# Eight columns' 47 rows end to end in three tiles of 128, a start without Nyquist DMAs, no clamp in the weights' conversion, and a new order of the steps

## The chip, the cores and the metric

One core of a Trainium2 chip. The time is the device time of one execution in microseconds (us). Matmuls run on TensorE (PE in the profile; PEld is its loading of weights), elementwise work on VectorE (DVE), ScalarE (ACT) and GpSimd (POOL), and most DMAs are issued by SyncE (SP). "fp32r" is the reduced form of float32 in which the large matmuls run.

## The reference

```python
# x: (8, 3008, 256) float32
X = np.fft.fft(x, axis=1)
X = np.fft.fft(X, axis=2)
h = X.real.astype(np.float32).reshape(8 * 3008, 256) @ w_in      # 256 -> 2048
g = np.where(h >= 1, h, np.where(h <= -1, 0.0, (h + 1) ** 2 / 4))
out = g @ w_out                                                  # 2048 -> 256
```

So: the real part of a two-dimensional Fourier transform of each batch, then a feed-forward layer with a piecewise activation. `w_in` and `w_out` arrive as float64, whose bits the kernel itself turns into float32.

## The kernel before

The transform over 3008 = 64 x 47 rows is done in two stages of matmuls. The host only rearranges x: row numbers become pairs (a of 64, b of 47), and each of eight tiles per batch holds 16 columns' values and their mirrored ones (the two halves of the tile's middle axis), which are added before stage 1 since only the real part of the result is wanted.

**Stage 1** (`stage1(b, q)`, L258, one call for each of 8 tiles q of batch b): `fold_x` adds the two halves on GpSimd (L129); for batch 0's first tile TensorE accumulates both halves instead. A tile has 96 partitions: two groups of 47 rows, each padded to 48. Four fp32 matmuls (L270) contract them with a block matrix `bm` of two cosine and sine blocks, 96 columns each, into one PSUM bank. Tile 0 has one more small matmul (L275) for the Nyquist column. Four copies of 64x192 carry the bank into `z` (L281 on VectorE for odd q of batch 0, L283 on ScalarE otherwise). **Stage 2** (`stage2(b, h)`, L308, six calls) contracts over the 64 and splits the result into high and low fp32r halves `pqh` (ScalarE, L165) and `pql` (VectorE, L166). `nyquist(b)` (L288) makes 24 rows of 64 for the Nyquist column; they go to DRAM, and `nyquist_rows` (L300) loads each of three chunks back, spread over 128 partitions. Batch 0 uses ScalarE's DMA queue for the first of these, the other batches SyncE's.

The rest of the transform over 256 is folded into the weights: `fold_w_in(f4, m)` (L233) multiplies the converted `w_in` by cosine or sine matrices (fp32 matmuls of 512 columns, L237) and splits the result into `wh` and `wl`; the sine half's first row becomes `delta`, which goes through DRAM to lie across partitions (`fold_delta`, L254; group 0 on ScalarE's queue).

**Conversion of weights.** There are 16 jobs of 128x512 float64 values: jobs 0, 1, 4, 5, 8, 9, 12, 13 of `w_in`, the others of `w_out`. `magnitude(n)` (L188) scales the high word on ScalarE (L199, by 2^112) and the low word (L201, or VectorE at L210 for jobs 0 and 1). `assemble(n)` (L204) clamps the scaled word from below (L211), shifts and merges the low word (L212), and puts the sign in (L214). Jobs from 6 on keep the scaled word in the PSUM bank that the transform also uses. `split_w_out(n)` (L220) makes high and low halves of `w_out`, the low one on GpSimd for jobs 2 and 3 and on VectorE for the others.

**Units.** Batch b, chunk k of 3 (482 or 512 columns) and feature tile f of 16 make one unit: `gemm1` (six fp32r matmuls, L368), then `us` and two `h` on VectorE (L371 to L374), relu and square on ScalarE (L381, L382), the larger of two on VectorE (L383), the high half `gh` on ScalarE (L384), the low half `gl` on GpSimd (L387), and four units later (`LAG`) `gemm2` (twelve matmuls, L411, into four accumulator banks). There are 48 units to a batch, 384 in all. Batch 0 goes over its chunks twice, for the first and then the last eight feature tiles.

**Order.** `LOADS` is the order of SyncE's first loads (the first two raws on ScalarE's queue), `START` the order on the four compute engines before unit 0, and `STEPS` what is added before a unit of batch 0. Letters: c converts (e and v: its two functions by themselves), p a piece of the transform of batch 0 (0 to 7 stage 1, 8 the Nyquist rows, 9 to 14 stage 2), a and b the two halves of a fold, o a split of `w_out`, l a load of a raw, k the clearing of a row, w filling matmuls, r `fold_delta` and the Nyquist rows. For the first four units TensorE keeps program order; elsewhere a scheduler places instructions by priority and its own model. Each later batch's transform of 15 pieces is spread over the units of the batch before it; in batch 0 it begins at unit `FIRST_DFT`, and its loads at `FIRST_LOAD`.

## Time and profile before

| | us |
|---|---|
| median of three runs | 1760.84 (1759.97 to 1761.49) |
| the profiled execution | 1763.07 |
| its span, first to last instruction | 1761.3 |

In the profile a row of the timeline has its start, its duration, engine, line and operation, the tile written and the tiles read, a count, and in brackets how long its engine was idle before it and what ended that. A row of a group has the count, the busy time and the mean duration in ns, then the idle time before it and its releasers. A row of the stages has the stretch, its length, each engine's busy time with the number of its instructions in brackets, the granted clock of TensorE, and the DMAs. Matmuls are pipelined: durations overlap, and the distance of two starts is what one of them costs.

### The profile page before, as it was taken

Reading aid. Unit: us, or ns where it says so; the run is one execution under the profiler, and the core shown is the slowest. Engines: PE = TensorE matmul, PEld = TensorE weight load, DVE = VectorE, ACT = ScalarE, POOL = GpSimd, SP = SyncE. Lnnn points to the kernel's source line nnn. Section 1 sums busy time; section 2 is a strip of 40 time slices with the busy share of each in tenths; the row PEclk is TensorE's granted clock in tenths of the full one; section 3 lists DMA queues with packets and bytes.
Section 4 is the critical chain, followed back from the end, with each engine's and each line's share of the span. In section 5 each row is a group of like instructions: output and inputs, shape, how many; then the busy total and the mean of one; then the engine's idle time right before and its main releaser. Section 6 shows DMA issues by size and latency. Waiting matters only on the chain.

```text
span 1761.3 us, 21722 instructions
## 1 busy us (share of the span) xinstructions
PE 1731.3 (98%) x7894; PEld 1413.0 (80%) x7894; DVE 1415.2 (80%) x1706; ACT 1351.2 (77%) x1587; POOL 1209.8 (69%) x853
## 2 busy tenths in 40 slices
PE   8999999999999999999999999999999999999999
PEld 4766788888888888888888888888888888888877
DVE  5888788788887887878877788777888778888887
ACT  5777877787777877787777877778778787777776
POOL 3556867876668766677666876677666766667775
PEclk9999999999999999999999999999999999999999
DMA  7023321110010100110001100011000001000000
GB/s 230 22 73 103 104 99 43 37 53 31 1 52 27 53 31 1 60 41 31 31 9 52 50 28 25 33 37 49 20 25 34 1 23 35 8 25 6 18 25 25
DMA packets 32084, 72.54 MB, mean 41 GB/s; under 512 B 5092, under 2 KB 10340, under 8 KB 31976
## 3 DMA queue, kind: packets, MB, share of 16 engines
...
q14 instruction: 46, 0.38, 0.1%
...
## 4 chain that ended last, share of the span: by engine, by line
PE 78%; ACT 4%; POOL 4%; DVE 3%; issue 2%; ACTq 0%; POOLq 0%
PE acc L411 49%; PE uv L368 24%; POOL gl L387 3%; DVE h L383 3%; PE s L270 2%; PE s L318 2%; ACT gh L384 2%; ACT a L382 2%; ACT a L381 1%; ACT z L283 0%; POOL y L129 0%; DVE h L373 0%; DVE h L374 0%; PE ny L290 0%; PE s L275 0%
## 5 line engine op out<-in xcount | busy, mean ns | idle before, releaser
L387 POOL TENSOR_TENSOR gl<-h,gh 128x512 fp32r<-128x512 f32 (+1 forms) x765 | 1089.1, 1447 | 491.7 <-ACT gh L384 435.0
L383 DVE SCALAR_TENSOR_TENSOR h<-a,h 128x1024 f32<-128x1024 f32 (+1 forms) x385 | 586.0, 1522 | 224.8 <-ACT a L382 223.1
L384 ACT ACTIVATE gh<-h 128x1024 fp32r<-128x1024 f32 (+1 forms) x385 | 400.7, 1041 | 349.3 <-DVE h L383 337.3
L411 PE MATMUL acc<-gh,woh 128*128 128x512 f32 (+1 forms) x1536 | 610.7, 398 | 7.2 <-ACT gh L384 4.6
L411 PE MATMUL acc<-gl,woh 128*128 128x512 f32 (+1 forms) x1536 | 605.0, 394 | 6.9 <-POOL gl L387 6.7
L411 PE MATMUL acc<-gh,wol 128*128 128x512 f32 (+1 forms) x1536 | 600.5, 391 | 0.0
L381 ACT ACTIVATE a<-h,half 128x1024 f32<-128x1024 f32 (+1 forms) x385 | 431.5, 1121 | 20.4 <-DVE h L374 18.4
L382 ACT ACTIVATE a<-a 128x1024 f32<-128x1024 f32 (+1 forms) x385 | 398.9, 1036 | 7.3
L411 PEld LDWEIGHTS acc<-gl,woh 128*128 128x128 f32 x1536 | 289.8, 189 | 75.0 <-POOL gl L387 14.4
L411 PEld LDWEIGHTS acc<-gh,woh 128*128 128x128 f32 x1536 | 290.2, 189 | 69.8 <-ACT gh L384 6.7
L411 PEld LDWEIGHTS acc<-gh,wol 128*128 128x128 f32 x1536 | 290.3, 189 | 59.6 <-issue 1.2
L373 DVE TENSOR_TENSOR h<-us,uv 128x512 f32<-128x512 f32 (+1 forms) x384 | 259.5, 676 | 67.2 <-POOL gl L387 26.6
L368 PE MATMUL uv<-pqh,wh 128*128 128x512 f32 (+1 forms) x768 | 302.8, 394 | 2.1 <-DVE h L374 1.4
L368 PE MATMUL uv<-pql,wh 128*128 128x512 f32 (+1 forms) x768 | 301.3, 392 | 0.0
L368 PE MATMUL uv<-pqh,wl 128*128 128x512 f32 (+1 forms) x768 | 300.4, 391 | 0.0
L371 DVE SCALAR_TENSOR_TENSOR us<-nyb,delta,uv 128x512 f32<-128x512 f32 (+1 forms) x384 | 278.8, 726 | 23.3 <-PE uv L368 18.3
L374 DVE TENSOR_TENSOR h<-us,uv 128x512 f32<-128x512 f32 (+1 forms) x384 | 256.2, 667 | 0.0
L368 PEld LDWEIGHTS uv<-pqh,wh 128*128 128x128 f32 x768 | 145.1, 189 | 40.9 <-DVE h L374 5.7
L368 PEld LDWEIGHTS uv<-pql,wh 128*128 128x128 f32 x768 | 144.9, 189 | 30.9 <-DVE pql L166 0.4
L368 PEld LDWEIGHTS uv<-pqh,wl 128*128 128x128 f32 x768 | 145.1, 189 | 29.7
L129 POOL TENSOR_TENSOR y<-x 96x512 f32<-96x512 f32 x56 | 100.2, 1789 | 11.1 <-PE s L270 7.5
L283 ACT ACTIVATE z<-s 64x192 f32<-64x192 f32 x240 | 81.3, 339 | 8.6 <-PE s L275 3.5
...
## 6 DMA issues: line engine op xcount, KB each, us to landing
x<-in_x_dram SPq DMA_DIRECT2D x64, 384.0 KB, 3.4
...
```

The costliest lines, as they stand in the source:

```text
L129: nc.gpsimd.tensor_tensor(y, t[:, 0], t[:, 1], op=ALU.add)
L283: nc.scalar.activation(dst, src, AF.Copy)
L368: nc.tensor.matmul(t[:, :n], w[m][:, cols], r[:, m, :n], start=(j == 0), stop=(j == 2))
L371: nc.vector.scalar_tensor_tensor(us, nyb[b, k][:, :n], delta[:, f : f + 1], uv[0], op0=ALU.mult, op1=ALU.add)
L373: nc.vector.tensor_tensor(h[:, 0], us, uv[1], op=ALU.subtract)
L374: nc.vector.tensor_tensor(h[:, 1], us, uv[1], op=ALU.add)
L381: nc.scalar.activation(a[:, sl], h[:, sl], AF.Relu, bias=half, scale=0.5)
L382: nc.scalar.activation(a[:, sl], a[:, sl], AF.Square)
L383: nc.vector.scalar_tensor_tensor(h[:, sl], a[:, sl], 1.0, h[:, sl], op0=ALU.min, op1=ALU.max)
L384: nc.scalar.activation(gh[:, sl], h[:, sl], AF.Copy)
L387: eng.tensor_tensor(gl[:, sg], h[:, sg], gh[:, sg].bitcast(F32), op=ALU.subtract)
L411: nc.tensor.matmul(acc[:, :n], w[:, f, wc], g[:, sg], start=(first and j == 0), stop=(last and j == 2))
```

## The change

1. **Stage 1.** Eight columns' 47 rows lie end to end, 376 rows in three tiles of 128 partitions. Each of three matmuls covers the columns that have rows in its tile: 3, 4 and 3 of them, 144, 192 and 144 outputs that overlap in the bank and accumulate there. A tile of x is 128 x 2 x 384 instead of 96 x 2 x 512.
2. **Batch 0's first Nyquist rows.** `nyquist_spread` makes chunk 0's rows on 128 partitions by eight matmuls whose stationary operand is one column of `z` repeated; `first_delta` turns group 0's row by four matmuls of one partition. The DMAs for these go, and so does ScalarE's queue: all loads are SyncE's.
3. **Conversion.** ScalarE scales by 2^-112, the clamp goes, and the sign is put in by another pair of bit operations. `w_out` results of jobs from 6 on are written into the raw tile, and all splits of `w_out` take GpSimd.
4. **Order.** New `LOADS`, `START` and `STEPS`; steps come after a unit's first half instead of before it; TensorE no longer keeps program order in the first units; batch 1's loads and transform begin at units 24 and 28 instead of 21 and 25.

```diff
+KT = 3
+XW = KT * P
+SPANS = [(k * P // NBB * 2 * NC, (min((k + 1) * P, 8 * NBB) - 1) // NBB * 2 * NC + 2 * NC) for k in range(KT)]
+BM = np.cumsum([0] + [hi - lo for lo, hi in SPANS])
...
-LOADS = "x0 l0 x1 l1 m0 x2 x3 x4 x5 x6 x7 l4 l5 l2 l3 l6 l7"
-START = "c0 c1 p0 w2 p1 p8 b0 p2 p3 p4 p5 p6 r0 e4 p7 k0 a0 p9 p10 e5 v4 e2 v5 v2 e3 v3"
-NEXT = ""
-MANUAL_UNITS = 4
+LOADS = "l0 x0 l1 m0 x1 x2 x3 x4 x5 x6 x7 l4 l5 l2 l3 l6 l7"
+START = "e0 v0 e1 v1 p0 b0 a0 p1 p8 p2 d0 p3 p4 p5 p6 e4 v4 p7 s0 p9 p10 e5 v5 k0 b1 e2 v2 e3 v3"
 STEPS = {
-    0: "o2",
-    1: "b1 a1 o3 p11",
-    2: "p12",
-    3: "p13 p14 l8 l9",
-    4: "c6 o6",
-    5: "c7 o7",
-    6: "l10",
-    9: "c8",
-    11: "c9 l11",
-    13: "b2 a2 c10 o10 l12",
-    15: "c11 o11 l13",
-    17: "c12 l14",
-    19: "c13 l15",
-    20: "c14 o14",
-    21: "b3 a3",
-    22: "c15 o15",
+    0: "a1 o2",
+    3: "o3",
+    4: "p11 e6 v6 l8 l9",
+    5: "p12",
+    6: "o6 e7 l12",
+    7: "v7 p13",
+    8: "o7",
+    9: "p14 e8",
+    10: "v8 l13",
+    11: "c9",
+    13: "b2",
+    14: "a2",
+    15: "c12 l10",
+    16: "l11",
+    17: "c13",
+    18: "l14",
+    19: "b3",
+    20: "a3",
+    21: "c10 l15",
+    22: "o10",
+    23: "c11",
+    24: "o11",
+    25: "c14",
+    26: "o14",
+    29: "c15",
+    30: "o15",
 }
-FIRST_LOAD, FIRST_DFT = 21, 25
+FIRST_LOAD, FIRST_DFT = 24, 28
...
-POOL_JOBS = (2, 3)
-LEAST = float(2.0**97)
+POOL_JOBS = (2, 3, 6, 7, 10, 11, 14, 15)
-SCALAR_LOADS = 2
+VECTOR_COPIES = (2, 4, 6)
...
-        pin(nc.scalar.activation(t, high.bitcast(F32), AF.Abs, scale=2.0**112))
+        pin(nc.scalar.activation(t, high.bitcast(F32), AF.Abs, scale=2.0**-112))
...
-        eng.tensor_scalar(t, t, LEAST, None, op0=ALU.max)
         nc.vector.scalar_tensor_tensor(bits, bits, 3, low, op0=ALU.logical_shift_left, op1=ALU.bitwise_or)
-        w = f32s.setdefault(n, t).bitcast(U32)
-        nc.vector.scalar_tensor_tensor(w, high, 0x7FFFFFFF, bits, op0=ALU.bitwise_or, op1=ALU.bitwise_and)
+        if n not in f32s:
+            f32s[n] = low.bitcast(F32)
+        w = f32s[n].bitcast(U32)
+        nc.vector.scalar_tensor_tensor(w, high, 0x80000000, bits, op0=ALU.bitwise_and, op1=ALU.bitwise_or)
...
+    def first_delta():
+        t = drows[0]
+        pt = fft_bank(0, "dps")[:, : 4 * NA].rearrange("p (i n) -> p i n", i=4)
+        for i in range(4):
+            nc.tensor.matmul(pt[:, i], t[:, i * P : (i + 1) * P], half[:1].to_broadcast([1, NA]), start=True, stop=True)
+        nc.scalar.activation(delta[:, :4], pt[:, :, 0], AF.Copy, scale=2.0)
...
-        for i in range(GPC):
+        for k, (lo, hi) in enumerate(SPANS):
             for j, part in enumerate(y):
-                lhs = part[:, i * P : (i + 1) * P]
-                mm = nc.tensor.matmul(pt[:, i], lhs, bm[:96, :], start=(j == 0), stop=(j == len(y) - 1))
+                at = k, j
+                mm = nc.tensor.matmul(
+                    pt[:, lo:hi],
+                    part[:, k * P : (k + 1) * P],
+                    bm[:, BM[k] : BM[k + 1]],
+                    start=at == (0, 0),
+                    stop=at == (KT - 1, len(y) - 1),
+                    skip_group_check=True,
+                )
...
-                if b == 0 and q % 2:
+                if b == 0 and q in VECTOR_COPIES:
                     nc.vector.tensor_copy(dst, src)
...
+    def nyquist_spread():
+        pt = fft_bank(0, "nys").rearrange("p (c d) -> p c d", d=NA)
+        for c in range(8):
+            lhs = zt[0][:, c, P : P + 1].to_broadcast([P, P])
+            nc.tensor.matmul(pt[:, c], lhs, rm[:, :NA], start=True, stop=True)
+        nyb[0, 0] = sb.tile([P, CH], F32, tag="nyb", name="nyb_0_0", bufs=4)
+        nc.scalar.activation(nyb[0, 0].rearrange("p (c d) -> p c d", d=NA), pt, AF.Copy)
...
             gemm1(i)
+            activate(i)
+            run_steps(STEPS.get(i, ""))
```

More of the change, by code (lines that the diff above doesn't have):

```diff
@@ L140, in fft_ffn_kernel @@
     bm, rm = (cs[:, _OFF[i] : _OFF[i + 1]] for i in range(2))
-    cm = sb.tile([P, _OFF[6] - _OFF[2]], F32, tag="y", name="cm", bufs=3)
+    cm = sb.tile([P, _OFF[6] - _OFF[2]], F32, tag="nyb", name="cm", bufs=4)
     mats = [[cm[:, (2 * m + h) * P : (2 * m + h + 1) * P] for h in range(2)] for m in range(2)]
@@ L183, in load_w @@
             src = w_out[at[0] * m : (at[0] + 1) * m, :].bitcast(U32).rearrange("(f p) x -> p f x", p=P)
-        queue = nc.scalar if n < SCALAR_LOADS else nc.sync
-        queue.dma_start(raw.rearrange("p e two -> p (e two)").rearrange("p (f x) -> p f x", f=src.shape[1]), src)
+        nc.sync.dma_start(raw.rearrange("p e two -> p (e two)").rearrange("p (f x) -> p f x", f=src.shape[1]), src)
         raws[n] = raw
@@ L242, in fold_w_in @@
         nc.scalar.activation(t, pt[:1, :], AF.Copy)
-        drows[f4] = dr.tile([1, CH], F32, tag="drow", name=f"drow_{f4}", bufs=2)
-        (nc.sync if f4 else nc.scalar).dma_start(drows[f4], t)
+        drows[f4] = t
+        if f4:
+            row = dr.tile([1, CH], F32, tag="drow", name=f"drow_{f4}", bufs=2)
+            nc.sync.dma_start(row, t)
+            nc.sync.dma_start(delta[:, f4 * 4 : f4 * 4 + 4], row.rearrange("o (i p) -> p (o i)", p=P))
         split(wh[m][:, cols], wl[m][:, cols], pt)
@@ L252, in clear_row @@
             nc.gpsimd.memset(w[1][:1, f4 * CH : (f4 + 1) * CH].bitcast(F32), 0.0)
-    def fold_delta(f4):
-        row = drows.pop(f4).rearrange("o (i p) -> p (o i)", p=P)
-        (nc.sync if f4 else nc.scalar).dma_start(delta[:, f4 * 4 : f4 * 4 + 4], row)
+    def first_delta():
[4 more added lines that the diff above has]
+        nc.scalar.activation(delta[:, :4], pt[:, :, 0], AF.Copy, scale=2.0)
     def stage1(b, q):
@@ L294, in nyquist @@
         row = dr.tile([NC, NA], F32, tag="row", name=f"nyr_{b}", bufs=2)
-        (nc.sync if b else nc.scalar).dma_start(row, t)
+        nc.sync.dma_start(row, t)
         rows[b] = row
-        if b:
-            nyquist_rows(b, range(NCHUNK))
+        nyquist_rows(b, range(0 if b else 1, NCHUNK))
+    def nyquist_spread():
[5 more added lines that the diff above has]
+        nc.scalar.activation(nyb[0, 0].rearrange("p (c d) -> p c d", d=NA), pt, AF.Copy)
     def nyquist_rows(b, ks):
@@ L369, in gemm1, with hidden @@
             uv.append(t[:, :n])
+        acts[i] = uv
+    def hidden(i):
+        b, k, f, *_ = units[i]
+        n = WIDTH[k]
+        uv = acts[i]
         us = sb.tile([P, CH], F32, tag="us", name=f"us_{i}", bufs=2)[:, :n]
@@ L374, in gemm1, with squares, halves, larger @@
         nc.vector.tensor_tensor(h[:, 1], us, uv[1], op=ALU.add)
-        a = sb.tile([P, 2, CH], F32, tag="a", name=f"a_{i}", bufs=3)[:, :, :n]
-        gh = sb.tile([P, 2, CH], F32R, tag="gh", name=f"gh_{i}", bufs=4)[:, :, :n]
-        gl = sb.tile([P, 2, CH], F32R, tag="gl", name=f"gl_{i}", bufs=4)[:, :, :n]
-        for sl in (slice(0, 2),) if i < n_units - 1 else (slice(0, 1), slice(1, 2)):
-            nc.scalar.activation(a[:, sl], h[:, sl], AF.Relu, bias=half, scale=0.5)
-            nc.scalar.activation(a[:, sl], a[:, sl], AF.Square)
-            nc.vector.scalar_tensor_tensor(h[:, sl], a[:, sl], 1.0, h[:, sl], op0=ALU.min, op1=ALU.max)
-            nc.scalar.activation(gh[:, sl], h[:, sl], AF.Copy)
+        acts[i] = h, sb.tile([P, 2, CH], F32, tag="a", name=f"a_{i}", bufs=3)[:, :, :n]
+    def squares(i, sl=slice(0, 2)):
+        h, a = acts[i]
+        nc.scalar.activation(a[:, sl], h[:, sl], AF.Relu, bias=half, scale=0.5)
+        nc.scalar.activation(a[:, sl], a[:, sl], AF.Square)
+    def halves(i):
+        b, k, *_ = units[i]
+        n = WIDTH[k]
+        return tuple(
+            sb.tile([P, 2, CH], F32R, tag=tag, name=f"{tag}_{i}", bufs=4)[:, :, :n] for tag in ("gh", "gl")
+        )
+    def larger(i, gh, sl=slice(0, 2)):
+        h, a = acts[i]
+        nc.vector.scalar_tensor_tensor(h[:, sl], a[:, sl], 1.0, h[:, sl], op0=ALU.min, op1=ALU.max)
+        nc.scalar.activation(gh[:, sl], h[:, sl], AF.Copy)
+    def low_halves(i, gh, gl):
+        h, _ = acts[i]
         for sg in range(2):
@@ L388, in gemm1, with activate @@
         acts[i] = gh, gl
+    def activate(i):
+        hidden(i)
+        gh, gl = halves(i)
+        for sl in (slice(0, 2),) if i < n_units - 1 else (slice(0, 1), slice(1, 2)):
+            squares(i, sl)
+            larger(i, gh, sl)
+        low_halves(i, gh, gl)
     accs = []
@@ L454, in fft_ffn_kernel @@
         "w": fill,
-        "r": lambda n: (fold_delta(0), nyquist_rows(0, range(NCHUNK))),
+        "s": lambda n: nyquist_spread(),
+        "d": lambda n: first_delta(),
     }
```

46 lines of the change are left out of this document (18 added, 28 removed).

## The prediction

> **What bounds the kernel now.** I read the page's busy times first, then the table of stages, then the timeline of the start, then the groups of instructions.
>
> ```profile
> PE 1731.3 (98%) x7894; PEld 1413.0 (80%) x7894; DVE 1415.2 (80%) x1706; ACT 1351.2 (77%) x1587; POOL 1209.8 (69%) x853
> ```
> ```profile
> core 0: us, PE busy (x) PEld busy (x) DVE busy (x) ACT busy (x) POOL busy (x), PEclk, DMA share, GB/s
> 24.30:41.30 17.00, 10.22 (x40) 5.75 (x39) 11.35 (x18) 9.81 (x17) 4.08 (x3) 0.80 0.60 208
> 41.30:104.00 62.70, 57.99 (x253) 44.54 (x252) 52.65 (x74) 48.98 (x59) 36.01 (x31) 1.00 0.12 38
> 104.00:160.00 56.00, 50.12 (x191) 35.45 (x190) 48.75 (x65) 40.45 (x48) 28.71 (x26) 0.97 0.28 84
> 160.00:245.00 85.00, 81.26 (x394) 66.37 (x395) 69.10 (x83) 69.16 (x96) 65.82 (x46) 1.00 0.31 100
> 245.00:460.00 215.00, 215.00 (x1007) 179.36 (x1006) 176.73 (x213) 167.37 (x196) 152.47 (x107) 1.00 0.13 43
> ```
>
> The last row is a whole batch: TensorE never idles, 1007 matmuls in 215.00 us, 0.2135 us each. Seven batches look like that, so there only fewer or shorter matmuls help. The four rows above it are batch 0, with all the weights' conversions. They hold 40 + 253 + 191 + 394 = 878 matmuls, worth 878 x 0.2135 = 187.5 us at the steady pace, and take 220.7: some 33 us are lost, of which 17.00 - 40 x 0.2135 = 8.5 lie in the first row and about 25 in the other three. Idle time alone (21 us) hides part of this, since a waiting matmul counts as busy. These 33 us and the matmuls of the transform are all that the change can reach.
>
> **Part 1, stage 1's matmuls.** Each fp32 matmul shows as two instructions. Before: 4 matmuls of 96 columns per tile. After: 3 matmuls of 144, 192 and 144 columns (spans of 3, 4 and 3 columns' 48 outputs). So 8 instructions become 6, but 384 columns become 480.
>
> ```profile
> L270 PE MATMUL s<-cs,y 96*128 96x96 f32 x448 | 58.1, 272 | 2.5 <-ACT z L283 2.5
> L318 PE MATMUL s<-cs,z 128*128 128x128 f32 x384 | 50.7, 275 | 0.0
> ```
> ```profile
> 45.27 1.05 PE L318 MATMUL s<-cs,z 128*128 128x128 f32 x8
> 301.19 1.03 PE L270 MATMUL s<-cs,y 96*128 96x96 f32 x8
> ```
> ```profile
> 22.99 0.19 PEld L237 LDWEIGHTS wps<-cv,cm 128*128 128x128 f32 x1 [0.24 <-issue]
> 23.42 0.19 PEld L237 LDWEIGHTS wps<-cv,cm 128*128 128x128 f32 x1 [0.24 <-issue]
> ```
>
> Spacing from these: 96 columns (1.03 - 0.272) / 7 = 0.108 us, 128 columns (1.05 - 0.275) / 7 = 0.111 us, so between 96 and 128 columns nothing depends on columns: the loading of 128 weight columns, the same in both, sets the pace. At 512 columns the spacing is 23.42 - 22.99 = 0.43 us, 0.84 ns a column: the streaming sets it. I take the larger of 0.11 us and 0.84 ns a column: 0.121, 0.161 and 0.121 us. After: 2 x (0.121 + 0.161 + 0.121) = 0.81 us a tile. Before: 8 x 0.108 to 0.111 = 0.87 to 0.89. Gain 0.06 to 0.08; 0.07 x 56 tiles of batches 1 to 7, all beside a TensorE that never waits: **-3.9 us** (3.3 to 4.6). Evictions of stage 1 keep shape and count. GpSimd's folds go from 512 to 384 columns; it is busy 69% of the span and nobody on TensorE waits for it in those batches, so that is worth nothing there.
>
> **Part 2, the start up to the first GEMM2.**
>
> ```profile
> 0.73 0.39 SPq L139 DMA_DIRECT2D cs<-in_cst_dram  x1
> 9.07 0.69 ACT L199 ACTIVATE cv<-raw 128x512 f32<-128x512 f32 x1 [3.37 <-DMA raw<-in_moe_w_in_dram]
> 12.03 2.31 PE L437 MATMUL warm<-warm 128*128 128x512 f32 x4
> 18.09 1.26 POOL L129 TENSOR_TENSOR x<-x 96x512 f32<-96x512 f32 x1 [0.25 <-DMA x<-in_x_dram]
> 19.55 1.26 POOL L129 TENSOR_TENSOR x<-x 96x512 f32<-96x512 f32 x1 [0.20 <-DMA x<-in_x_dram]
> 22.54 0.69 ACT L283 ACTIVATE z<-s 64x192 f32<-64x192 f32 x2
> 23.46 0.67 ACT L199 ACTIVATE cv<-raw 128x512 f32<-128x512 f32 x1 [0.24 <-issue]
> 24.34 2.02 PE L318 MATMUL s<-cs,z 128*128 128x128 f32 x16
> 28.54 0.38 PE L368 MATMUL uv<-pql,wh 128*128 128x482 f32 x1
> 32.26 0.72 DVE L371 SCALAR_TENSOR_TENSOR us<-nyb,delta,uv 128x482 f32<-128x482 f32 x1 [4.21 <-DMA nyb<-nyr]
> 34.90 5.76 PE L237 MATMUL wps<-cv,cm 128*128 128x512 f32 x8 [5.97 <-DVE cv L214]
> 41.30 0.46 PE L368 MATMUL uv<-pqh,wh 128*128 128x482 f32 x1
> 42.70 0.38 PE L411 MATMUL acc<-gh,woh 128*128 128x482 f32 x1
> ```
> ```profile
> x<-in_x_dram SPq DMA_DIRECT2D x64, 384.0 KB, 3.4
> ```
> ```profile
> L212 DVE SCALAR_TENSOR_TENSOR cv<-cv,raw 128x512 uint32<-128x512 uint32 x6 | 4.1, 687 | 0.1
> ```
>
> Before, unit 0's first VectorE operation waits for the Nyquist rows' DMA until 32.26. Raw 5's conversion stands behind it in VectorE's order, and TensorE, in program order for four units, stands behind that from 28.54 to 34.90. Its 8 fold matmuls then take 5.76 us where 8 x 0.43 is 3.4, with the stage's clock at 0.80. After, TensorE makes these rows and delta's first columns itself, so no DMA is waited for.
>
> What is late next is the input. x 6 and x 7 land 1.46 us apart (384 KB). The bytes ahead of x 7 are the same as before (constants, two raws, eight x), now on one queue instead of two, so I leave x 7 at 19.55. Raw 1 goes third: 1520 KB at 384 KB per 1.46 us is 5.8 us after the first issue at 0.73, and the way to landing adds about 1.9 (3.4 us for an x less its own 1.46): 8.4, against 9.07 or before. That matters because both halves of the first fold now stand ahead of the second stage-1 piece on TensorE, and all pieces would queue behind a late raw 1. With x 7 at 19.55 its fold takes 1.26 x 384/512 = 0.95 and piece 7 0.8: 21.3. But piece 7's evictions now stand on ScalarE behind raw 4's two conversions (they were VectorE's). Raw 4, 512 KB behind x 7, lands at 19.55 + 1.95 = 21.5; two conversions of 0.67 give 22.9; four evictions of 0.345 give 24.2. So stage 2 starts at 24.2, against 24.34: no gain up to here, and the dropped fill (2.31 us) and the added 24 small instructions (24 x 0.11 = 2.6 us) both lie in time in which TensorE waits for x. Then raw 5's conversion follows the second piece's eviction on ScalarE, at 27.0 to 28.3, VectorE finishes it by 29.7 (two of 0.69), and the fold ends at 31.4 with its second half soon behind, against 34.90 to 40.7: 5 us ahead. The upper end is the whole 8.5 us of this row, the lower end nothing. I take **-5 us**.
>
> [...]
>
> **Part 3, VectorE's work in batch 0's units.**
>
> ```profile
> L211 DVE TENSOR_SCALAR cps<-cps 128x512 f32<-128x512 f32 x10 | 6.9, 694 | 0.3 <-ACT cps L199 0.3
> L166 DVE TENSOR_TENSOR wol<-cps,woh 128x512 fp32r<-128x512 f32 x6 | 4.1, 681 | 0.0
> L166 POOL TENSOR_TENSOR wol<-cv,woh 128x512 fp32r<-128x512 f32 x2 | 2.8, 1418 | 8.5 <-ACT woh L165 8.5
> L383 DVE SCALAR_TENSOR_TENSOR h<-a,h 128x1024 f32<-128x1024 f32 x255 | 384.5, 1508 | 145.8 <-ACT a L382 144.6
> ```
> ```profile
> PEld acc L411 <- POOL gl L387: 14.4, 19, 1.5
> PEld acc L411 <- ACT gh L384: 6.7, 5, 2.1
> ```
>
> GEMM2's weight loads wait for gl and gh, which both wait for VectorE's h. Each conversion puts a clamp, two assemblies and (half of them) a split on VectorE between units: the ten clamps (6.9 us) go, and six splits (4.1 us) go to GpSimd, 11.0 us in all. The steps also come singly where two shared an iteration. The lost time beyond the start is 25 us; the bounds are nothing and all of it. I take the 11.0 that leave VectorE: **-11 us**. GpSimd gains 6 x 1.418 = 8.5 us, where it is idle for 31% of the span. Two clamps on GpSimd and four VectorE ones of the start go besides; they lie beside the input wait. What this costs if the cover is gone is a rival below.
>
> **Part 4, the denser transform.** Batch 1's 15 pieces fit into 20 units (28 to 47) where they had 23, and the last four conversions come at iterations 21 to 29, beside them. ScalarE's evictions hold up stage 1 there:
>
> ```profile
> PEld s L270 <- ACT z L283: 4.1, 4, 1.7
> ```
>
> Four such waits of about 1 us; I add **+1.5 us** (0 to 4). The next loads of x go from unit 21 to 24, four units ahead of use as before.
>
> **The sum.** -3.9 - 5 - 11 + 1.5 = -18.4 us. The profiled execution took 1763.07 us (span 1761.3), so it becomes 1744.7; the runs' median is 1760.84, 2.2 below it, so 1742.4. I say 1742.
>
> **The rivals.**
> - The start gains nothing: x and raw 4 set its end and unit 0's chain to GEMM2 is as long as before. For it: stage 2 starts at the same time. Against: 5.97 us of wait with a named cause that goes. 1760.84 - 3.9 - 11 + 1.5 = 1747.4.
> - VectorE's relief is hidden: it was busy 52.65 of 62.70 us, 84%, and the units' own chain sets the pace. 1760.84 - 3.9 - 5 + 1.5 = 1753.4.
> - Slower: the six splits on GpSimd collide with VectorE. These two rows are the same operation, the first beside two gl and the subtraction for the Nyquist column on GpSimd:
>
> ```profile
> 183.15 3.01 DVE L383 SCALAR_TENSOR_TENSOR h<-a,h 128x964 f32<-128x964 f32 x1 [0.55 <-ACT a L382]
> 187.22 1.15 DVE L383 SCALAR_TENSOR_TENSOR h<-a,h 128x964 f32<-128x964 f32 x1
> ```
>
> It took 1.86 us longer. A split that delays gl by 1.418 and stretches h by 1.86 costs 3.3 us; six cost 19.7 where only the clamps' 6.9 are saved: 1760.84 - 3.9 - 5 - 6.9 + 1.5 + 19.7 = 1766.2. It decides from the fifth of six splits that falls wholly on the path (14.3 / 3.28 = 4.4). Against: LAG is 4 units, and the steady batches hide 8 folds each on the same engine. [...]
> - Stage 1 costs by the column even when narrow, 0.108/96 = 1.13 ns: 480 x 2 x 1.13 = 1.08 us a tile, 0.21 more, +12 us for 56 tiles: 1760.84 - 5 - 11 + 1.5 + 12 = 1758.3. Against: 96 and 128 columns have the same spacing.
>
> **How the numbers follow.** Forecast 0.55, start without gain 0.12, hidden relief 0.14, collisions 0.09, cost by column 0.04, and 0.06 for more than forecast (below 1730: the whole 8.5 and 20 of the 25 us). The range runs from 1730 to 1757: it takes in the forecast's own bounds and the first two rivals, and leaves out 0.09 + 0.04 + 0.06 = 0.19. A measurement tells 0.2%, 3.5 us, from no change. Faster by more: 0.55 + 0.12 + 0.14 + 0.06 = 0.87, less 0.01 for the edge: 0.86. Within: 0.05. Slower: 0.09.
>
> **What would show it.** Steady batches near 214.4 us where they had 215, and stage-1 instructions about 0.12 and 0.16 us apart: part 1. No wait of VectorE for the Nyquist rows of chunk 0, first fold of the second weight group by about 32 us, first GEMM2 by 38: part 2. Fewer GEMM2 waits for gl and gh before 245 us: part 3. h over 2.5 us beside splits on GpSimd with waits for gl after each would show the collisions. The forecast fails if the stage-1 piece takes over 0.9 us, if raw 1 lands past 11 us, or if unit 0's chain on VectorE runs behind the conversions of raws 2 and 3.

## The result and the profile after

The changed kernel takes **1739.03 us**, the median of 4 runs (1738.74 to 1741.40); beside it the kernel before took 1761.16 (1759.97 to 1761.93). The ratio is 0.9878, 95% interval 0.9861 to 0.9895: faster by 22.1 us, where 18.4 was forecast. The profiled execution took 1738.74 us with a span of 1736.9.

The page's busy times of the changed kernel:

```profile
PE 1719.6 (99%) x7784; PEld 1409.7 (81%) x7784; DVE 1374.7 (79%) x1682; ACT 1353.9 (78%) x1593; POOL 1216.1 (70%) x857
```

TensorE is busy for 12 us less and idle for 17 us instead of 30. VectorE has given up 40 us of busy time. The table of stages, over the same five stretches and with the same columns as before (PE, PEld, DVE, ACT and POOL, then the granted clock, the share of the DMA engines and GB/s):

```profile
24.30:41.30 17.00, 13.54 (x56) 9.00 (x57) 13.41 (x22) 13.20 (x21) 5.06 (x5) 0.95 0.28 93
41.30:104.00 62.70, 61.66 (x269) 48.84 (x269) 56.82 (x73) 53.30 (x62) 44.58 (x34) 0.99 0.11 33
104.00:160.00 56.00, 55.16 (x236) 43.45 (x235) 47.28 (x65) 47.15 (x58) 44.11 (x34) 1.00 0.31 100
160.00:245.00 85.00, 81.42 (x388) 66.55 (x387) 65.65 (x83) 68.12 (x94) 60.24 (x45) 1.00 0.35 118
245.00:460.00 215.00, 214.98 (x987) 178.25 (x986) 171.17 (x208) 165.65 (x194) 151.56 (x107) 1.00 0.10 34
```

More matmuls fit in each of the first three stretches (56 for 40, 269 for 253, 236 for 191); the third, where the last conversions used to crowd, gains most. Batch 0's end and the steady batch show fewer because the transform has fewer instructions.

For what follows I cut the span at three starts: the first GEMM2, the first GEMM2 of batch 1 (the 577th matmul into acc), and the last matmul. The timelines, of the kernel before first, then of the changed one (start, duration):

```profile
293.18 0.47 PE L411 MATMUL acc<-gh,woh 128*128 128x482 f32 x1
...
1757.29 0.40 PE L411 MATMUL acc<-gl,woh 128*128 128x512 f32 x1
```
```profile
39.25 0.48 PE L466 MATMUL acc<-gh,woh 128*128 128x482 f32 x1 [1.58 <-ACT gh L428]
...
274.29 0.48 PE L466 MATMUL acc<-gh,woh 128*128 128x482 f32 x1
...
1732.71 0.39 PE L466 MATMUL acc<-gl,woh 128*128 128x512 f32 x1
```

The start was 42.70 and is 39.25: -3.45. Batch 0 was 293.18 - 42.70 = 250.48 and is 235.04: -15.44. Batches 1 to 7 were 1464.11 and are 1458.42: -5.69. Together that is 24.6; the medians differ by 22.1 since the profiled execution of the kernel before was 1.9 us above its median. The forecast had -5, -9.5 (VectorE's relief and the denser transform together) and -3.9. So all three moved the right way, and batch 0 moved by 6 us more than forecast. Whether the named causes did it, the experiments say.

### The profile page after: what moved, and what is told of

It is laid out like the page before. It is cut to its first block, busy times and chain, and to the rows that moved or that the text cites. A ratio compares the mean times of both kernels' runs of the same rounds, so it can differ in the third digit from the quotient of the medians.

```text
span 1736.9 us, 21505 instructions
## 1 busy us (share of the span) xinstructions
PE 1719.6 (99%) x7784; PEld 1409.7 (81%) x7784; DVE 1374.7 (79%) x1682; ACT 1353.9 (78%) x1593; POOL 1216.1 (70%) x857
## 4 chain that ended last, share of the span: by engine, by line
PE 81%; ACT 7%; POOL 4%; DVE 4%; issue 2%; DMA 0%; ACTq 0%; POOLq 0%; DVEq 0%
PE acc L466 51%; PE uv L398 25%; POOL gl L434 3%; DVE h L427 2%; ACT a L416 2%; PE s L348 2%; ACT gh L428 2%; PE s L285 2%; ACT a L415 2%; POOL y L140 1%; ACT z L305 0%; DVE h L409 0%; PE wps L247 0%; DVE h L410 0%; ACT o L477 0%
## 5 line engine op out<-in xcount | busy, mean ns | idle before, releaser
L434 POOL TENSOR_TENSOR gl<-h,gh 128x512 fp32r<-128x512 f32 (+1 forms) x765 | 1106.4, 1469 | 461.9 <-ACT gh L428 419.1
L427 DVE SCALAR_TENSOR_TENSOR h<-a,h 128x1024 f32<-128x1024 f32 (+1 forms) x385 | 563.0, 1463 | 249.8 <-ACT a L416 248.5
L140 POOL TENSOR_TENSOR y<-x 128x384 f32<-128x384 f32 x56 | 86.8, 1550 | 9.2 <-PE s L285 4.9
```

The costliest lines, as they stand in the source:

```text
L140: nc.gpsimd.tensor_tensor(y, t[:, 0], t[:, 1], op=ALU.add)
L427: nc.vector.scalar_tensor_tensor(h[:, sl], a[:, sl], 1.0, h[:, sl], op0=ALU.min, op1=ALU.max)
L434: eng.tensor_tensor(gl[:, sg], h[:, sg], gh[:, sg].bitcast(F32), op=ALU.subtract)
```

## The experiments

Every row is one kernel. "Batch 0" and "batches 1 to 7" are cut as above, in the profiled execution. "Half clock" gives the start and length of the stretches, up to the last matmul, in which the granted clock was 0.5. The kernel before took between 1761.2 and 1763.2 us on the chips of these runs; the four fastest kernels (after, a_oldsteps, a_nyqdma, a_best), on three chips, lie between 1738.4 and 1739.6. So I subtract medians, take nothing under some 3 us between chips for a difference, and the ratios with their intervals stand beside.

| kernel | median us | ratio to before (95%) | first GEMM2 | batch 0 | batches 1 to 7 | half clock |
|---|---|---|---|---|---|---|
| before | 1761.16 | 1 | 42.70 | 250.48 | 1464.11 | 31.8, 6.8; 147.9, 3.4 |
| after | 1739.03 | 0.9878 (0.9861 to 0.9895) | 39.25 | 235.04 | 1458.42 | 39.7, 3.4 |
| b_wide2 | 1754.96 | 0.9958 (0.9941 to 0.9974) | 40.57 | 249.32 | 1459.41 | 29.9, 6.8; 146.0, 3.4 |
| a_narrow | 1753.46 | 0.9937 (0.9921 to 0.9952) | 45.09 | 239.16 | 1463.80 | 19.3, 13.7; 50.0, 3.4 |
| a_narrow128 | 1752.98 | 0.9948 (0.9933 to 0.9963) | 45.04 | 238.32 | 1463.90 | 18.3, 13.7; 45.6, 3.4 |
| a_narrow_nod | 1745.89 | 0.9901 (0.9882 to 0.992) | 39.34 | 239.42 | 1462.95 | 157.5, 3.4; 178.0, 3.4 |
| a_nyqdma | 1739.55 | 0.9872 (0.9859 to 0.9886) | 40.30 | 234.79 | 1457.82 | 24.2, 3.4 |
| a_both | 1746.30 | 0.9902 (0.989 to 0.9915) | 39.09 | 241.83 | 1458.56 | 39.2, 3.4; 158.7, 3.4 |
| a_clamps | 1744.35 | 0.9903 (0.9885 to 0.9921) | 39.09 | 240.13 | 1459.37 | 39.2, 3.4 |
| a_dvesplit | 1744.57 | 0.9898 (0.9883 to 0.9913) | 39.85 | 239.70 | 1459.26 | 157.0, 6.8 |
| a_oldsteps | 1738.52 | 0.9861 (0.9848 to 0.9873) | 39.87 | 233.51 | 1458.46 | none |
| a_bothold | 1750.81 | 0.9933 (0.9919 to 0.9947) | 39.98 | 246.22 | 1458.63 | 167.5, 3.4 |
| a_early | 1741.02 | 0.9883 (0.987 to 0.9897) | 39.93 | 237.95 | 1459.39 | 44.5, 3.4; 160.6, 3.4 |
| a_best | 1738.36 | 0.9865 (0.9851 to 0.9878) | 38.89 | 235.07 | 1458.42 | 39.0, 3.4 |

### Stage 1's shape, alone and undone

**a_narrow** is the changed kernel with the old stage 1: x in 96 partitions of two columns' rows, four matmuls of 96 columns.

```diff
-        t = sb.tile([P, 2, XW], F32, tag=tag, name=f"x_{b}_{q}", bufs=bufs)
+        t = sb.tile([96, 2, CH], F32, tag=tag, name=f"x_{b}_{q}", bufs=bufs)
...
-        for k, (lo, hi) in enumerate(SPANS):
+        for i in range(GPC):
             for j, part in enumerate(y):
...
+                lhs = part[:, i * P : (i + 1) * P]
+                mm = nc.tensor.matmul(pt[:, i], lhs, bm[:96, :], start=(j == 0), stop=(j == len(y) - 1))
```

> The changed kernel with the old stage 1: tiles of 96 partitions, four matmuls of 96 columns, x in rows of 4 KB on 96 partitions. By the sum's first term it loses 3.9 us in batches 1 to 7 (0.56 us a batch), so 1743 against 1739.0, and a little more if the input's landing sets the start. The rival: in the changed kernel the steady batches gained next to nothing (211.0 to 211.2 us between two batches' first GEMM2, 211.16 before in the undisturbed ones) because a wait for an eviction took the piece's gain back; then the batches stay within 0.2 us and whatever is lost is lost ahead of the first GEMM2, where x 7 would land near 19.5 instead of 16.5: up to 3 us.

It took 1753.46 us (1746.41 to 1754.90 over 6 runs), 14 us more than the changed kernel. Batches 1 to 7 lose 5.4 us and batch 0 loses 4.1. The start loses 5.8, and comes out later than that of the kernel before; neither the forecast (1743) nor its rival had that. **b_wide2** goes the other way: the kernel before with the new stage 1 and nothing else (the weights' matrices share another buffer, so that the wider tiles fit: without that, in b_wide, the kernel needs 142.84 KB a partition where 141.375 are left).

```diff
+KT = 3
+XW = KT * P
...
-        t = sb.tile([96, 2, CH], F32, tag=tag, name=f"x_{b}_{q}", bufs=bufs)
+        t = sb.tile([P, 2, XW], F32, tag=tag, name=f"x_{b}_{q}", bufs=bufs)
...
-        for i in range(GPC):
+        for k, (lo, hi) in enumerate(SPANS):
```

> The kernel before with the new stage 1 alone (the fold's matrices moved to the Nyquist rows' buffers, as in the changed kernel). Undoing stage 1 in the changed kernel cost 5.8 us up to the first GEMM2, 4.1 in batch 0 and 5.4 in batches 1 to 7. If these add to the rest of the change, the kernel before gains the same: first GEMM2 near 39, time near 1747. If the wait for the Nyquist rows' DMA hides the earlier x, the start stays at 42 to 43 and the time is 1751 to 1753. By my sum's first term alone: 1757.

It took 1754.96 us, 7.7 less than the kernel before on the same chip: 4.7 of it in batches 1 to 7, 2.1 in the start, 1.2 in batch 0. That is nearest to the sum's first term alone (1757): what the shape cost when undone in the changed kernel does not come back in the old one. The piece itself (eight instructions of stage 1, in after six), in the timelines of before and of after:

```profile
300.97 0.39 PE L368 MATMUL uv<-pql,wh 128*128 128x482 f32 x1
...
302.00 0.47 PE L411 MATMUL acc<-gh,woh 128*128 128x482 f32 x1
302.31 0.38 PE L411 MATMUL acc<-gh,wol 128*128 128x482 f32 x1
```
```profile
294.79 0.38 PE L398 MATMUL uv<-pql,wh 128*128 128x482 f32 x1
295.01 0.98 PE L285 MATMUL s<-cs,y 128*128 128x144 f32 x6
295.73 0.48 PE L466 MATMUL acc<-gh,woh 128*128 128x482 f32 x1
296.04 0.38 PE L466 MATMUL acc<-gh,wol 128*128 128x482 f32 x1
```

From the matmul ahead of a piece to the second one behind it is 1.34 us here before and 1.25 after; the medians over the 46 pieces behind batch 1's first GEMM2 are 1.340 and 1.264. The new instructions are 0.122 and 0.162 us apart. That is -0.076 a piece, 4.3 us for 56, where 0.07 and 3.9 were forecast. Ten of the 56 pieces run in batch 0, ahead of that GEMM2, so of the 5.7 us of batches 1 to 7 the pieces' own time makes 3.5.

The rest does not lie evenly. Batches 1 and 2 run at the same pace with and without the change: 211.16 and 211.16 us before, 211.02 and 211.15 after. Of the 0.6 us that eight pieces save, most goes back to a wait that the old kernel did not have. The waits of TensorE's weight loads in the middle batches (waited for, total us, times, longest), of before from 715 to 1141 us and of after from 696 to 1118:

```profile
PEld uv L368 <- DVE h L374: 3.6, 6, 1.2
```
```profile
PEld acc L466 <- ACT o L477: 0.9, 2, 0.5
```

At a change of chunk GEMM2 is now earlier than the eviction that frees its bank. Batches 3 and 4, in turn, gain 1.9 and 1.8 us: there the kernel before has the waits for h of the first line, and after has none. VectorE's h of 964 elements has become shorter on the mean (groups of before from 504 to 1352 us, of after from 485 to 1329 us: busy us, mean ns):

```profile
L383 DVE SCALAR_TENSOR_TENSOR h<-a,h 128x964 f32<-128x964 f32 x64 | 105.2, 1643 | 46.1 <-ACT a L382 45.9
```
```profile
L427 DVE SCALAR_TENSOR_TENSOR h<-a,h 128x964 f32<-128x964 f32 x65 | 91.5, 1407 | 52.6 <-ACT a L416 52.6
```

The h of 1024 elements has not (1493 and 1496 ns). Over the same stretches GpSimd's fold went from 1888 to 1624 ns on the mean. One of the long ones in each batch runs beside a fold in both kernels, here in before and then in after:

```profile
718.84 2.17 DVE L383 SCALAR_TENSOR_TENSOR h<-a,h 128x964 f32<-128x964 f32 x1 [1.17 <-ACT a L382]
718.68 1.30 POOL L129 TENSOR_TENSOR y<-x 96x512 f32<-96x512 f32 x1
```
```profile
700.07 1.88 DVE L427 SCALAR_TENSOR_TENSOR h<-a,h 128x964 f32<-128x964 f32 x1 [1.17 <-ACT a L416]
699.89 1.03 POOL L140 TENSOR_TENSOR y<-x 128x384 f32<-128x384 f32 x1
```

The fold is 0.27 us shorter, and this h 0.29. But that is one h of a batch's sixteen. Most of the mean's 236 ns comes from the others that were long: 14 of the 64 took over 1.7 us before (2.16 to 2.80, each beside a fold, a gl or both), and 4 after, all of the kind shown; the other 60 of after take 1.61 us at most. Both means go with stage 1's shape: b_wide2 has the short pair (1412 and 1585 ns), and a_narrow_nod (below), which has all of the change but the shape, the long one, 1601 and 1890 ns. No run shortened the fold alone, so that the fold brings the other h out of step too is argued, not shown. I had costed that fold at nothing.

The start of a_narrow needed two more kernels. **a_narrow128** pads its x to 128 partitions, so that every DMA reaches all of them, and computes as a_narrow does.

```diff
-        "x": xp.reshape(NB, XC, 96, 2, CH),
+        "x": np.pad(xp.reshape(NB, XC, 96, 2, CH), ((0, 0), (0, 0), (0, 32), (0, 0), (0, 0))),
```

> The changed kernel with the old stage 1, but x padded to 128 partitions, so that its DMA writes 512 KB in rows of 4 KB over 128 partitions instead of 384 KB over 96; compute uses the first 96. If the 96 partitions made x slow (packets of 4 KB took 254 to 289 ns there, 159 ns in the raws' loads on 128), x tiles land 1.3 us apart although they are a third larger, and the first GEMM2 comes at 40 to 42 us instead of 45.1; time 1749 to 1750. If the length of the rows or the single queue made it slow, they land 2.2 us apart and the first GEMM2 comes at 48 or later, time 1757.

The stretch from 10 to 15 us, when little but x is loaded, in before, a_narrow, a_narrow128 and after (the last number is GB/s):

```profile
10.00:15.00 5.00, 4.94 (x31) 3.49 (x29) 2.57 (x3) 1.76 (x6) 3.70 (x3) 1.00 1.04 260
```
```profile
10.00:15.00 5.00, 5.00 (x23) 2.94 (x22) 1.01 (x2) 3.05 (x9) 2.97 (x3) 1.00 1.03 231
```
```profile
10.00:15.00 5.00, 5.00 (x23) 2.94 (x21) 1.58 (x3) 3.42 (x9) 4.24 (x4) 1.00 1.02 419
```
```profile
10.00:15.00 5.00, 5.00 (x21) 2.89 (x20) 1.57 (x3) 3.21 (x9) 4.56 (x5) 1.00 1.04 414
```

The DMA engines are busy throughout in all four (their share is above 1.0). Tiles of 96 partitions come at 231 to 260 GB/s, tiles of 128 at 414 to 419, whether their rows hold 4 KB (a_narrow128) or 3 KB (after). So in these loads the rate went with the partitions and not with the row length: with rows of 4 KB it was 231 on 96 partitions (a_narrow) and 419 on 128 (a_narrow128). By their number alone the rate would be 0.75 of 414, an estimate of 310 GB/s, and the measured one is lower; no run shows why.

And yet a_narrow128's first GEMM2 is at 45.04, no earlier than a_narrow's. Its stretches, and those of **a_narrow_nod**, say what held it. That kernel leaves out a_narrow128's first_delta, eight instructions with one weight row each, and fetches delta's first columns by DMA, on SyncE's queue.

```diff
-START = "e0 v0 e1 v1 p0 b0 a0 p1 p8 p2 d0 p3 p4 p5 p6 e4 v4 p7 s0 p9 p10 e5 v5 k0 b1 e2 v2 e3 v3"
+START = "e0 v0 e1 v1 p0 b0 a0 p1 p8 p2 p3 p4 p5 p6 e4 v4 p7 s0 p9 p10 e5 v5 k0 b1 e2 v2 e3 v3"
...
-        if f4:
+        if True:
             row = dr.tile([1, CH], F32, tag="drow", name=f"drow_{f4}", bufs=2)
```

> The changed kernel with the old stage 1 and x on 128 partitions, and with delta's first columns through DRAM on SyncE's queue instead of the eight one-row matmul instructions between pieces 2 and 3. With them TensorE's clock fell to half at 18.3 us, for 13.7 us, though TensorE had hardly waited, and the first GEMM2 came at 45.0. If the one-row matmuls between narrow pieces made that stretch too idle for the clock, it stays whole, and the first GEMM2 comes near 39 to 40, time 1746 to 1747. If the narrow pieces alone did it, the clock falls again and the first GEMM2 stays near 44 to 45, time 1752.

The stretches by granted clock (third number from the end) of a_narrow128, then of a_narrow_nod:

```profile
14.90:18.30 3.40, 3.40 (x28) 3.07 (x28) 2.11 (x5) 1.81 (x7) 3.35 (x3) 1.00 1.03 411
18.30:31.90 13.60, 13.60 (x66) 13.60 (x66) 4.63 (x11) 6.44 (x16) 2.30 (x4) 0.50 0.94 343
```
```profile
18.30:31.90 13.60, 12.33 (x84) 10.02 (x82) 9.20 (x19) 9.01 (x21) 1.96 (x3) 1.00 0.97 313
```

In a_narrow128 the clock is halved for 13.7 us, 66 instructions pass where 84 do at the full clock, and VectorE and ScalarE wait for them. Ahead of it TensorE was not idle: 3.40 of 3.40 us busy, with these groups:

```profile
L287 PE MATMUL s<-cs,x 96*128 96x96 f32 x18 | 2.7, 287 | 0.0
L272 PE MATMUL dps<-half,drow 1*128 1x64 f32 x8 | 1.1, 276 | 0.0
L307 PE MATMUL ny<-cs,z 128*24 128x64 f32 x2 | 0.3, 238 | 0.0
```

With the eight one-row instructions gone, the clock stays whole, the first GEMM2 comes 5.7 us earlier and the kernel takes 7.1 us less. The other runs agree: the granted clock over the whole execution is 0.994 to 0.996 in a_narrow128's four and 0.998 to 1.000 in a_narrow_nod's. The instructions of 96 columns alone don't do it, since a_narrow_nod has 48 of them in a row at full clock:

```profile
16.61 5.60 PE L287 MATMUL s<-cs,x 96*128 96x96 f32 x48
```

All the half-clock stretches of the table last 3.4, 6.8 or 13.7 us, and this one came behind a stretch with no idle time. The changed kernel has the eight instructions too, between wider ones, and keeps its clock through this stretch (1.00 from 14.9 to 31.9 us). So little work per instruction is what I read from it, but how little is enough was not tried, and leaving the eight out also moved what stands ahead of them: that is argued, not shown.

With stage 1 undone and the clock whole in the start, the shape is worth 0.1 us there, 4.5 in batches 1 to 7 (1462.95 against 1458.42) and 4.4 in batch 0 (239.42 against 235.04). Much of the last is probably the clock again, which is halved twice for 3.4 us in batch 0 of this profile: two of a_narrow_nod's four runs took 1743.90 and 1744.23, some 3.5 us less than the profiled one (1747.55). a_narrow128, with one such stretch in batch 0 as after has, makes 238.32, 3.3 more than after. So in batch 0 the shape is worth somewhere between 1 and 4 us.

### The Nyquist rows

**a_nyqdma** puts the rows of chunk 0 and delta's first columns back on DMAs, in the new order.

```diff
+        row = dr.tile([1, CH], F32, tag="drow", name=f"drow_{f4}", bufs=2)
+        (nc.sync if f4 else nc.scalar).dma_start(row, t)
+        drows[f4] = row
...
-        "s": lambda n: nyquist_spread(),
-        "d": lambda n: first_delta(),
+        "r": lambda n: (
+            nc.scalar.dma_start(delta[:, :4], drows[0].rearrange("o (i p) -> p (o i)", p=P)),
+            nyquist_rows(0, range(1)),
+        ),
```

> The changed kernel with batch 0's first Nyquist rows and delta's first columns through DRAM again, by ScalarE's DMA queue as before; the new order, stage 1 and conversion stay. Second term of the sum: VectorE's first operation of unit 0 waits for the rows' DMA, the fold of raws 4 and 5 stands behind it or beside it, and the first GEMM2 comes 3 to 5 us later than 39.25, with TensorE's clock halved for longer. Rival, the input landing earlier was the whole gain: x is out of the queue by 16.5 us, the rows land before 29 us when unit 0's operation runs anyway, and the first GEMM2 stays within 1 us of 39.25.

It took 1739.55 us: no difference. The first GEMM2 comes 1.05 us later, not 3 to 5, behind a stretch of 3.4 us at half clock, and batch 0 takes no longer. VectorE's timeline there:

```profile
30.03 0.69 DVE L224 SCALAR_TENSOR_TENSOR cv<-raw,cv 128x512 uint32<-128x512 uint32 x1
30.64 0.71 DVE L407 SCALAR_TENSOR_TENSOR us<-nyb,delta,uv 128x482 f32<-128x482 f32 x1
```

The operation that waited 4.21 us before follows the conversion ahead of it without a wait. The rows' DMA, issued at 20.50 us, ends at 30.02 in this trace, before that conversion is done. In b_wide2, which has the old order, the operation does wait, and the fold stands behind it:

```profile
29.89 0.72 DVE L382 SCALAR_TENSOR_TENSOR us<-nyb,delta,uv 128x482 f32<-128x482 f32 x1 [3.08 <-DMA nyb<-nyr]
32.52 6.00 PE L241 MATMUL wps<-cv,cm 128*128 128x512 f32 x8 [4.85 <-DVE cv L218]
```

There the rows' DMA ends at 29.76, no later. So in the new order the wait is gone with or without the DMAs, because raw 5's conversion now stands ahead of unit 0's operation. Whether rows from TensorE would have done as much in the old order was not run. **a_best** asks whether more is to be had: a_oldsteps (below), with the last piece and the spread ahead of raw 4's conversion.

```diff
-START = "e0 v0 e1 v1 p0 b0 a0 p1 p8 p2 d0 p3 p4 p5 p6 e4 v4 p7 s0 p9 p10 e5 v5 k0 b1 e2 v2 e3 v3"
+START = "e0 v0 e1 v1 p0 b0 a0 p1 p8 p2 d0 p3 p4 p5 p6 p7 s0 e4 v4 p9 p10 e5 v5 k0 b1 e2 v2 e3 v3"
```

> The changed kernel with the iterations of the old STEPS, and in START the seventh piece and the Nyquist spread ahead of raw 4's conversion, so that ScalarE moves the piece's result out before it converts. Stage 2 begins when the piece's evictions end, 1.2 us earlier (two conversions of 0.66), so the first GEMM2 near 38.6 instead of 39.9; time 1737 to 1738. If unit 0's chain on VectorE behind the conversions of raws 2 and 3 sets the end of the start, nothing moves: 1738.5.

Stage 2 starts at 23.30 us, against 25.05 in a_oldsteps and 24.44 in the changed kernel, and the first GEMM2 comes at 38.89, 0.98 earlier than in a_oldsteps (1.3 were forecast). Batch 0 then takes 1.6 us more, with 3.4 us at half clock that a_oldsteps does not have. In the changed kernel the first GEMM2 is only 0.36 later, behind the conversions of raws 2 and 3 on VectorE. 1738.36 us cannot be told from either kernel.

### VectorE's work in batch 0

**a_clamps** puts the ten clamps back (at zero, which costs the instruction and changes no value), **a_dvesplit** the six splits onto VectorE, **a_both** both. **a_oldsteps** is the changed kernel with the old order of the steps between the units, each ahead of its unit, and **a_bothold** is a_oldsteps with both put back.

```diff
-POOL_JOBS = (2, 3, 6, 7, 10, 11, 14, 15)
+POOL_JOBS = (2, 3)
...
+        if n >= 6:
+            nc.vector.tensor_scalar(t, t, 0.0, None, op0=ALU.max)
```
```diff
-    0: "a1 o2",
-    3: "o3",
-    4: "p11 e6 v6 l8 l9",
+    0: "o2",
+    1: "a1 o3 p11",
+    2: "p12",
+    3: "p13 p14 l8 l9",
+    4: "c6 o6",
...
+        run_steps(STEPS.get(i, ""))
         if i < n_units:
...
             activate(i)
-            run_steps(STEPS.get(i, ""))
```

> The changed kernel with a clamp at zero (it changes no value) in jobs 6 to 15 on VectorE, ten of 0.69 us. Third term, first part: 6.9 us if all of it is on the path. With the splits on VectorE as well batch 0 lost 6.8 of 11.0 us, so in proportion 4.3 here: batch 0 near 239.3 between the first GEMM2s instead of 235.0. If what counts is when VectorE is full (the last conversions beside the next transform), all the loss lies after 155 us.

> The changed kernel with the six splits of w_out for jobs 6 to 15 on VectorE again (0.68 us each) instead of GpSimd (1.44 each). Third term, second part: 4.1 us, or in proportion 2.5: batch 0 at 237.5. The rival of collisions: GpSimd's splits block VectorE's larger-of-two and delay gl, so moving them back gains: batch 0 under 234.5.

> The changed kernel with VectorE's work in batch 0 put back: a clamp at zero (which changes no value) in jobs 6 to 15, ten of 0.69 us, and the six splits of w_out on VectorE instead of GpSimd. Third term of the sum: 11 us lost, 1750. If the gain of batch 0 came from the new order of the steps, which stays here, 1739 to 1742. If the splits on GpSimd collide with VectorE in the changed kernel, moving them back gains, and the sum is under 1746.

> The changed kernel with the iterations of the old STEPS and the steps ahead of a unit's first half again (START, the loads' order and the start of the next transform stay new). By the sum the order is worth nothing or 1.5 us the other way: 1738 to 1741. If batch 0's gain of 15 us came from the order, since steps no longer come two or more to an iteration: 1747 to 1754.

> The changed kernel with both VectorE's work (ten clamps, six splits) and the iterations of the old STEPS put back. Alone the work cost 6.8 us of batch 0 and the old iterations gained 1.5. If these add, batch 0 takes 240.3 us between the first GEMM2s. If the two stand in for each other (either spread steps or less work keeps VectorE from running full), together they cost far more than alone: 246 to 249 us, near the 249.3 of the kernel before with the new stage 1.

In batch 0 the clamps cost 5.1 us (forecast 4.3), the splits 4.7 (2.5), both 6.8; in the kernel's time 5.3, 5.5 and 7.3 (by the ratios 3.5 to 4.4). The old order of the steps alone costs nothing (233.51 against 235.04). But with the old order the two together cost 12.7 us (246.22 against 233.51) and 12.3 of the time. The third stretch, 104 to 160 us, of a_both and of a_bothold:

```profile
104.00:160.00 56.00, 52.22 (x213) 39.31 (x212) 51.54 (x70) 45.92 (x54) 35.16 (x28) 0.99 0.24 77
```
```profile
104.00:160.00 56.00, 50.46 (x197) 35.78 (x196) 49.01 (x66) 44.24 (x52) 34.26 (x28) 1.00 0.28 88
```

The changed kernel had x236 there, a_both x213, a_bothold x197, and the kernel before x191. What stands behind it are GEMM2's waits for gl, over the whole span, of a_both, of a_bothold and of after:

```profile
PEld acc L468 <- POOL gl L436: 10.7, 13, 3.2
```
```profile
PEld acc L458 <- POOL gl L426: 14.8, 16, 1.6
```
```profile
PEld acc L466 <- POOL gl L434: 1.9, 3, 0.9
```

a_oldsteps has 0.5 us of them. So the two measures stand in for one another: as I read it, steps that come singly spare the units a pair of conversions at once, and shorter steps spare them the same. With the work gone, the order is worth nothing; with the old order the work is worth 12. The six splits themselves (mean ns), on GpSimd in after and on VectorE in a_dvesplit:

```profile
L177 POOL TENSOR_TENSOR wol<-raw,woh 128x512 fp32r<-128x512 f32 x6 | 8.6, 1441 | 1.2 <-ACT woh L176 1.2
```
```profile
L177 DVE TENSOR_TENSOR wol<-raw,woh 128x512 fp32r<-128x512 f32 x6 | 6.1, 1020 | 0.1
```

Six on VectorE are 6.1 us, not the 4.1 of the prediction, but the mean hides two kinds: four took 0.68 to 0.88 us and two 1.50 and 1.69. And they are not the old splits. The old ones read the converted weight from the PSUM bank (cps), these from the raw tile in SBUF, which the change put in its place. Two of them that run beside gl on GpSimd, in before and in a_dvesplit:

```profile
150.36 0.68 DVE L166 TENSOR_TENSOR wol<-cps,woh 128x512 fp32r<-128x512 f32 x1
```
```profile
158.94 1.69 DVE L177 TENSOR_TENSOR wol<-raw,woh 128x512 fp32r<-128x512 f32 x1
```

b_wide2's one split beside gl took 0.68 too, and a_both and a_bothold have three of 1.56 to 1.79 beside GpSimd. So a_dvesplit, a_both and a_bothold put the splits back on VectorE in a form that can cost more than the old one. The loss of a_dvesplit lies elsewhere in the main, too. TensorE stands still for 4.54 us, with 6.8 us at half clock about the end of it, and GpSimd's fold had waited 3.13 us for a load of x shortly before:

```profile
151.50 1.01 POOL L140 TENSOR_TENSOR y<-x 128x384 f32<-128x384 f32 x1 [3.13 <-DMA x<-in_x_dram]
158.09 1.94 PE L285 MATMUL s<-cs,y 128*128 128x144 f32 x6 [4.54 <-POOL gl L434]
```

In after the longest such wait of the fold is 0.6 us. But a_oldsteps has one of 3.2 us without such a stop, so the link between the two is not shown, nor is what the splits alone are worth.

### The denser transform

**a_early** puts batch 1's first load and first piece back to units 21 and 25.

```diff
-FIRST_LOAD, FIRST_DFT = 24, 28
+FIRST_LOAD, FIRST_DFT = 21, 25
```

> The changed kernel with the next batch's loads and transform from units 21 and 25 again instead of 24 and 28. Fourth term of the sum: the denser transform costs 1.5 us (0 to 4), so batch 0 would take 233.5 us instead of 235.0 between the first GEMM2s. Rival: the earlier transform shares its PSUM bank and VectorE with the conversions of jobs 10, 11, 14 and 15, which come at iterations 21 to 29, and batch 0 gets 1 to 4 us longer.

1741.02 us: 1.5 more than a_nyqdma and 2.7 more than a_best on the same chip, less than can be told with certainty. In the trace batch 0 takes 2.9 us more, as the rival had it, but the profiled execution took 1743.51, the slowest of the four (the others 1740.54 to 1741.26), and has 3.4 us more at half clock. From 104 to 160 us TensorE gets 222 instructions done, where the later start has 236: the pieces that start earlier do so among the conversions. So the later, denser transform is no worse place; that it is a better one is not shown. It does wait: of TensorE's own waits from 104 to 245 us in after the largest is

```profile
PE s L285 <- DVE raw L224: 2.4, 2, 1.5
```

a piece whose bank is held by a conversion.

## Why the prediction was right, and where it was wrong

The time was forecast at 1742 (1730 to 1757) and is 1739.03. Faster was right, and so was the main mechanism, VectorE's work in batch 0. That the sum came so near is in part luck: the start gained less than its term and not for the reason given, the other two stretches more. The parts:

- **Part 1, right.** My estimate, "the larger of 0.11 us and 0.84 ns a column", gave 0.121 and 0.161; measured 0.122 and 0.162. That the weights' columns set the pace of narrow instructions has a sign in after: at 64 columns those with 128 weight columns start 0.112 us apart (L326), those with 24 start 0.094 apart (L312; medians). The rival "cost by column" fell. The -3.9 was for 56 pieces; the 46 that lie in batches 1 to 7 give -3.5, and these batches gained 5.7, b_wide2 alone 4.7. What I left out is that a shorter piece meets a wait for an eviction in some batches, and that the kernel before waits for VectorE's h in others, waits that went with the old shape. "A TensorE that never waits" was not so there, and "worth nothing there", on the folds, does not fit the runs, though no run changed the folds alone. The 215 us that I called a whole batch were the length of my window; from one batch's first GEMM2 to the next it was 211.16 us and is 211.0 to 211.2 in batches 1 and 2. The pace worked out from it, 0.2135 us, stands.
- **Part 2, size near by luck, cause wrong.** -3.45 against -5. The step that failed first is "I leave x 7 at 19.55": the load rate went from 260 to 414 GB/s. The timeline of after has all seven folds of x over by 17.51, on GpSimd:

```profile
10.44 7.07 POOL L140 TENSOR_TENSOR x<-x 128x384 f32<-128x384 f32 x7 [2.28 <-DMA x<-in_x_dram]
24.44 2.05 PE L348 MATMUL s<-cs,z 128*128 128x128 f32 x16 [0.75 <-ACT z L305]
```

  I had them end with x 7's at 19.55 + 0.95 = 20.5. Stage 2 still starts at 24.44, near the forecast 24.2, because ScalarE's conversions of raw 4 set it, and that much of the step held. But they begin at 21.76 because they stand behind an eviction, not because raw 4 lands at 21.5 as I had it. The second failure is the named cause, "no DMA is waited for": in the new order the time is the same with the DMAs back. Of the -3.45, b_wide2 has -2.1 from the shape of x alone, and undone in the new order (a_narrow_nod) the shape is worth 0.1: shape and order stand in for one another here. The first GEMM2 was to come by 38 and came at 39.25. The text had named the condition: unit 0's chain does run behind the conversions of raws 2 and 3, as VectorE's timeline shows. The last operation of raw 3's conversion is followed at once by the h from which the first GEMM2's gh comes:

```profile
36.37 0.68 DVE L224 SCALAR_TENSOR_TENSOR cv<-raw,cv 128x512 uint32<-128x512 uint32 x1
36.97 1.16 DVE L427 SCALAR_TENSOR_TENSOR h<-a,h 128x964 f32<-128x964 f32 x1
```

- **The clock behind the start, in no term of the sum.** Behind waits of TensorE of at most 1.58 us the clock is halved from 39.7 to 43.1 us in after:

```profile
36.30:39.70 3.40, 1.61 (x10) 1.39 (x11) 3.40 (x6) 3.30 (x6) 2.48 (x2) 1.00 0.00 0
39.70:43.10 3.40, 3.40 (x11) 2.72 (x9) 3.40 (x6) 3.37 (x5) 3.40 (x3) 0.50 0.00 0
```

  It cost little: a_oldsteps, with as little work on TensorE in the first of these stretches (1.57 us), has no half clock up to its last matmul and takes the same time. What tells the two apart is not known.
- **Part 3, right in mechanism; its size depends on the order.** -11.0 was the sum of the instructions removed. Put back into the changed kernel they cost 4 to 7, put back into the old order 12 to 13, with splits that read SBUF where the old ones read PSUM. GEMM2's waits for gl, the sign that I named, went from 13.6 to 1.2 us between 40 and 245 us. The rival "VectorE's relief is hidden" fell, in either order.
- **Part 4, not borne out.** +1.5 was forecast; undoing it gains nothing, and costs 2.9 us of batch 0 in the one trace, that of the slowest of four runs. I looked at the four waits among the pieces and not at what the pieces displaced where they stood before.
- **The collisions, the slower rival, fell.** Its sign was an h of over 2.5 us beside a split on GpSimd; in after the only two h beside a split took 1.16 and 1.22. Long splits there were on both engines: 1.50 and 1.69 us on VectorE in a_dvesplit, where the other four took 0.68 to 0.88, and 2.04 and 2.06 on GpSimd in after, beside those two h, where the other six took 1.30 to 1.33. What makes them long, no run shows. The gain of 4.7 us that a_dvesplit seems to show is mostly one stop of TensorE.
- **Not forecast at all:** stage 1's shape in batch 0, 1.2 us in the old order (250.48 against 249.32) and 1 to 4 in the new.

Batch 0 gained 15.4 us where 9.5 were forecast. From before through b_wide2, a_bothold and a_oldsteps to after, its stretch goes 250.48, 249.32, 246.22, 233.51, 235.04: 1.2 for the shape, 3.1 for all else but work and steps, 12.7 for clamps and splits, and -1.5 for the new steps. In another order of undoing the shares differ, as the 6.8 us of a_both shows, so no one share is the price of its part.

Taken one after the other by the ratios of the table, from before: the new shape 0.42%, then the new order of the start with the rows on TensorE and the later transform (a_bothold) 0.25%, scarcely clear of the intervals, then clamps and splits (a_oldsteps) 0.72%, then the new steps, nothing that can be told. One run of a_narrow took 1746.41 where the other five took over 1752; its granted clock was 0.999 where theirs was 0.993 to 0.995, so it lost the less to the clock. What stays open: what halves the clock, what the splits alone are worth, and what the raw tile as the place of the converted w_out does, since no run undid it.
